# Attention scores from tile 4 on as three float32r products instead of float32 products, and the order planned anew

## Chip, core and metric

The kernel runs on one core of one Trainium2 chip. The metric is the device time of one execution, in microseconds (us); less is better. All times below are of one core.

## What is computed

Attention with rotary positions over 4 batches, 8 heads, 576 positions and a head width of 64, and behind it a two-layer feed-forward network over the 2304 tokens (512 to 2048 to 512 columns). The reference, cut to its core:

```
q_rot, k_rot = rotate(q), rotate(k)
scores = scale * (q_rot @ k_rot.T)
attn = exp(scores - max(scores))
attn = attn / (sum(attn) + 1e-9)
x = (attn @ v)                     # heads side by side: 2304 x 512
h = x @ w_in
out = (max(h, 0) + alpha * min(h, 0)) @ w_out
```

## The kernel before

**Tiles and blocks.** The 2304 tokens are cut into 18 tiles of 128; two tiles make a block, nine blocks in all. A batch has 576 tokens, that is four and a half tiles, so tiles 4 and 13 (counted from 0) lie half in one batch and half in the next. The eight heads are taken as four pairs: the two heads of a pair lie on partitions 0 to 63 and 64 to 127 of the tiles of keys (`ks`) and queries (`qn`).

**One unit of attention** is one tile and one pair of heads. `keys` (L381) and `queries` (L602) load the raw data and its rotated copy (`kraw`, `qr`), multiply both by a table (`tab`) and add them up. `pair` (L627) makes the scores on TensorE: two halves of 288 columns times two heads, each one float32 product over 64 rows of the array (L638). Tiles 4 and 13 go through `half_pair` (L650): their 64 tokens of one batch, for both heads, are laid into one 128 x 128 stationary operand with zeros in the two other quarters (L658, L660), and two float32 products of 288 columns give the scores (L666). Then, for each head (`head`): VectorE takes the maximum (L690), ScalarE the exponential (L699), the weights are split into a high and a low float16 part (L707 or L354, L716), SyncE issues a DMA that transposes them (`pt<-pp`, L720), and 14 short TensorE products with the float16 values `vv` follow (L727). The values of a batch are loaded (L412), split and copied to a second place by eight DMAs (`vv<-vv`, L455). When a tile is through, it is normalised (L771), split and transposed by a DMA (`xt<-xs`, L804).

**The network** takes a block (256 tokens) through 16 groups of 128 hidden columns: twelve float16 products into `h` (L823), the leaky rectifier (L834, L837), a split of the result in a high part `gh` and a low part `gl` (L851, L854), and six float32r products of 512 columns (L861) that add into `pair` banks: high by high, high by low, low by high. The first two blocks use float32 products there (L817, L843), while the weights are prepared; tiles 0 and 1 also do the rest of their attention in float32 (L745, L751).

**What sets the order.** Nothing runs in the order in which it is written. Each operation is recorded with a due time and the engines that may take it, with a cost for each (`op`); `Plan.run` then goes through a model of the five engines and always gives a free engine the ready operation with the earliest due time. The due times are shifted by the numbers in the table `PRM`. What comes out is a fixed list for each engine, which works it off in that order and waits where an operand isn't there. SyncE issues all DMAs, in its list's order. The lines that matter for a pair's scores on TensorE, with the cost that the plan assumes for them in ns:

```python
nc.tensor.matmul(out=ps[h]()[:, x, :HS], lhsT=qn()[r, p], rhs=kt()[r, x * HS:(x + 1) * HS], start=True, stop=True)
...
op(at, {PE: PRM["tqk"]}, scores, kind=WIDE, reads=[(qn, p // 2 * 2), kt], writes=ps)
```

Of the kernel before, what the change touches and what calls it, by code (L numbers as in the profile page):

```python
# [31 lines left out]
    [80, 75, 60, 102, 170],  # L32
    [160, 160, 160, 160, 0],
]
PRM = {"pf": 2, "pc": 3.0, "si": 3.47, "sd": 7.38, "qd": 8.0, "qd0": 3.81, "vl0": 40.33, "wl": 12.02, "wl2": 15.99, "wb": 7.7, "wb2": 0.16, "ws": -0.8, "ws2": 0.93, "kl": 23.6, "vl": 20.33, "lead": 3.61, "flow": 6, "pen": -2.44, "ph": -1.15, "xlo": 3.07, "kd": 3.61, "pl": 0.16, "wlo": 3.44, "wg": 4.0, "bk": 1500, "lead1": 1.74, "ph0": 2.99, "nb": 1, "wh": 11.0, "lw": 2.44, "pvd": 2.98, "pw": 4.01, "la": 3, "lv": 1, "nks": 5, "nvv": 5, "ka": 3.0, "va": -0.1, "vc": -2.76, "vp": 1.38, "qa": 0.46, "qr": 184.66, "tqk": 1340, "l2d": 2.62, "tl2": 1400, "nos": 2, "nr": 2, "fo": 0, "fi": 4, "gh": 9.4, "gl": 11.01, "gh0": -1.64, "gl0": 3.28, "tp": 0, "nf": 2, "sh": 2.27, "sl": 2.28, "tl": 0, "wpe": 0, "vpe": 1, "wk": 5.0}


class Buf:
# [13 lines left out]
class Tag:  # L52
    def __init__(self, pool, bufs, shape, dt, name, tag=None):
        self.pool, self.bufs, self.all, self.opened = pool, bufs, [], 0
        self.make = lambda: pool.tile(shape, dt, name=name, tag=f"{tag or name}{self.opened % bufs}")

    def new(self):
        k = len(self.all)
# [182 lines left out]
def attention_moe(ctx: ExitStack, tc: tile.TileContext, q, k, v, w_in, w_out, alpha, tab, eye, out):  # L241
# [15 lines left out]
    nc = tc.nc  # L257
# [45 lines left out]
    wus_b = single("wus", [128, 1], F32)  # L303
    wmax_b = single("wmax", [128, KC // 2, NG], F32)
    wo_pool = ctx.enter_context(tc.tile_pool(name="wo_p", bufs=1))
    ks_T = tag("ks", PRM["nks"], [128, S], F32)
    vv_T = tag("vv", PRM["nvv"], [128, 2, NSEG + NH, D], F16)
    rk_T = tag("kraw", 2, [128, 2, S], F32)
    rv_T = tag("vraw", NP, [128, 2, NH, D], F32)
    qr_T = tag("qr", 2, [128, 2, NP, 128], F32)  # L310
    qn_T = tag("qn", 2, [128, NP, 128], F32)
    st_T = tag("st", 2, [128, NP], F32)
    e_T = tag("e", 2, [128, S], F32)
    pp_T = tag("pp", 3, [128, 2, S], F16)
# [61 lines left out]
        small(at, lambda: nc.vector.reciprocal(out=dst(), in_=dst()), writes=[dst_acc])  # L376


    ks = {}

    def keys(at, b, p):  # L381
        r, t = rk_T.new(), ks_T.new()
        ks[b, p] = t
# [8 lines left out]
        op(at - PRM["ka"], {POOL: t_pool(S), DVE: (t_dve(S), slow)},  # L392
           lambda e: ENG[e].tensor_tensor(out=t(), in0=r()[:, 0], in1=r()[:, 1], op=ALU.add),
           reads=[(r, 0), (r, 1)], writes=[t])

# [204 lines left out]
    qs = {}  # L600

    def queries(at, t):  # L602
        raw, qn = qr_T.new(), qn_T.new()
        qs[t] = qn
        parts = tiles[t]
        cuts = [[0], [2]] if t == 0 else [[0, 2]]
        op(at - (PRM["qd0"] if t == 0 else PRM["qd"]), {SP: t_dma(128 * 2 * NP * 128 * 4)}, lambda e: nc.sync.dma_start(out=raw(), in_=q[t]),
           writes=[(raw, (p[2], x)) for p in parts for x in (0, 2)])
        for n, xs in enumerate(cuts):
            c, w = slice(xs[0], xs[-1] + 2), 2 * len(xs) * 128  # L610
            late = at - PRM["qa"] + 0.1 * n
# [12 lines left out]

    sums, ys, xss, vos, xt = {}, {}, {}, {}, {}

    def pair(at, step, t, b, p, a, z, banks):  # L627
        kt, vt, qn = ks[b, p], vv[b, p], qs[t]
        if z - a < 128:
            return half_pair(at, t, b, p, a, z, banks[p % 2])  # L630
        ps = [x.new() for x in banks]


        def scores(e):
# [13 lines left out]
    qds, sts = {}, {}  # L648

    def half_pair(at, t, b, p, a, z, bank):  # L650
        kt, vt, qn = ks[b, p], vv[b, p], qs[t]
        if (t, a) not in qds:
            qd, sts[t, a] = qr_T.new(), st_T.new()
            qds[t, a] = qd
            for h in range(2):
                o, c = 64 * h, 64 - 64 * h
                op(at - 2, {POOL: 420, DVE: (t_dve(256, fast=True), 1)},
                   lambda e, o=o, c=c: ENG[e].memset(qd()[o:o + 64, 0, :, c:c + 64], 0.0), writes=[(qd, h)])  # L658
                op(at - 2, {ACT: t_act(256)},
                   lambda e, o=o: nc.scalar.activation(out=qd()[o:o + 64, 0, :, o:o + 64], in_=qn()[o:o + 64, :, a:z], func=ACTF.Copy),  # L660
                   reads=[(qn, 0), (qn, 2)], writes=[(qd, 2 + h)])
# [250 lines left out]
    def attention(i):  # L912
# [116 lines left out]
```

## Time and profile before

| | us |
|---|---|
| median of 3 runs (lowest, highest) | 676.44 (675.19, 678.43) |
| profiled execution, first to last instruction | 674.6 |
| lowest run over the profiled span | 0.6 |
| TensorE (PE) busy | 643.3 |
| its weight loads (PEld), beside the products | 480.3 |
| VectorE (DVE) busy | 471.6 |
| ScalarE (ACT) busy | 338.5 |
| GpSimd (POOL) busy | 218.7 |

The profiled execution's span is the only time that is given for it; the runs' times lie up to 3.8 us above it, the median 1.8 us. Busy time of PE overlaps within itself: a product's end is modelled, and the next begins before it. So what a group of products costs is read from the starts, not from the sum of the durations. A float32 product stands in the trace as two instructions, each with a weight load of its own (512 for the 256 products of L638); a float32r product stands there as one.

### The profile page before, as it was taken

How to read it: one execution, taken by the hardware profiler on the slowest of the kernel's cores; microseconds unless marked ns; L12 is line 12 of the kernel's file. 1: busy time of each engine (PE TensorE's matmuls, PEld its weight loads, DVE VectorE, ACT ScalarE, POOL GpSimd, SP SyncE). 2: the span in 40 equal slices, each digit the busy share in tenths (PEclk: the TensorE clock that was granted, in tenths of full speed). 3: DMA queues.
4: the chain of work that ended last, by engine and by line, in shares of the span. 5: the costliest groups of instructions: out<-in, count | busy, mean ns of one | idle time of the engine just before them, and what ended most of it. 6: DMA issues, size and time to landing. Idle time of an engine off the chain costs nothing.

```text
span 674.6 us, 13695 instructions
## 1 busy us (share of the span) xinstructions
PE 643.3 (95%) x5378; PEld 480.3 (71%) x5378; DVE 471.6 (70%) x754; ACT 338.5 (50%) x752; POOL 218.7 (32%) x178
## 2 busy tenths in 40 slices
PE   1998999999999999999989999999999999999997
PEld 1577766676666667777767777788777777778775
DVE  4889799875877767587759776777766665664332
ACT  4355357653646548445634555554555544543322
POOL 3793101103476636165514221123233232211000
PEclk9999999999999999999979999999999999999999
DMA  8962885866674545658686646674865546553000
GB/s 292 329 245 97 307 249 125 195 105 149 162 201 88 121 82 120 121 137 189 148 170 116 120 87 80 114 163 93 153 129 102 88 75 102 107 100 52 32 0 32
DMA packets 185840, 90.69 MB, mean 134 GB/s; under 512 B 168624, under 2 KB 172848, under 8 KB 185776
## 3 DMA queue, kind: packets, MB, share of 16 engines
q1 hardware_dynamic: 185776, 89.82, 58.8%
q8 instruction: 42, 0.69, 0.4%
q14 instruction: 22, 0.18, 0.1%
HBM read 41.56 MB, written 4.72 MB: 69 GB/s over the span
## 4 chain that ended last, share of the span: by engine, by line
PE 85%; DMA 7%; DVE 4%; ACT 2%; issue 1%; SPq 1%; POOL 0%; ACTq 0%; DVEq 0%
PE pair L861 22%; PE h L823 21%; PE pair L638 10%; PE v L727 8%; PE h L817 8%; PE pair L843 7%; DMA pt<-pp 4%; PE pair L745 3%; PE v L751 2%; DMA kraw<-in_k_dram 2%; PE pair L666 2%; PE pair L468 1%; DVE mx L690 1%; DMA qr<-in_q_dram 1%; DMA xt<-xs 1%
## 5 line engine op out<-in xcount | busy, mean ns | idle before, releaser
L823 PE MATMUL h<-xt,wi 128*128 128x256 f16 x1344 | 175.7, 275 | 1.1 <-DMA xt<-xs 0.7
L823 PEld LDWEIGHTS <-wi 128*128 128x128 f16 x1344 | 120.1, 98 | 43.0 <-issue 28.5
L699 ACT ACTIVATE e<-pair,mx 128x576 f32<-128x576 f32 x144 | 105.8, 738 | 83.0 <-DVE mx L690 81.8
L837 DVE SCALAR_TENSOR_TENSOR r<-r,beta,h 128x256 f32<-128x256 f32 x144 | 68.8, 478 | 94.1 <-ACT r L834 93.0
L834 ACT ACTIVATE r<-h 128x256 f32<-128x256 f32 x144 | 55.2, 383 | 145.2 <-PE h L823 106.7
L690 DVE TENSOR_REDUCE mx<-pair 128x1 f32<-128x576 f32 x144 | 103.3, 751 | 25.6 <-PE pair L638 21.9
L854 POOL TENSOR_TENSOR gl<-r,gh 128x256 fp32r<-128x256 f32 x69 | 56.4, 818 | 175.6 <-ACT gh L851 152.9
L716 DVE SCALAR_TENSOR_TENSOR pp<-e,pp 128x576 f16<-128x576 f32 x128 | 102.6, 811 | 11.2 <-ACT pp L707 9.5
L861 PE MATMUL pair<-wh,gh 128*128 128x512 f32 x224 | 97.0, 433 | 0.0
L861 PE MATMUL pair<-wh,gl 128*128 128x512 f32 x224 | 88.6, 395 | 0.0
L727 PEld LDWEIGHTS <-pt 128*128 128x128 f16 (+1 forms) x2016 | 71.9, 102 | 23.0 <-issue 12.3
L861 PE MATMUL pair<-wo,gh 128*128 128x512 f32 x224 | 87.7, 391 | 0.0
L727 PE MATMUL v<-vv,pt 128*128 128x64 f16 (+1 forms) x2016 | 78.1, 195 | 4.6 <-DMA pt<-pp 4.6
L638 PE MATMUL pair<-ks,qn 64*128 64x288 f32 x512 | 82.3, 433 | 0.0
L851 ACT ACTIVATE gh<-r 128x256 fp32r<-128x256 f32 x102 | 42.5, 417 | 52.0 <-DVE r L837 26.7
L817 PE MATMUL h<-xt,wi 128*128 128x256 f32 x256 | 66.7, 392 | 1.3 <-DVE xt L788 1.2
L638 PEld LDWEIGHTS pair<-ks,qn 64*128 64x128 f32 x512 | 46.9, 189 | 23.7 <-issue 12.1
L843 PE MATMUL pair<-wo,r 128*128 128x512 f32 x128 | 60.5, 598 | 0.0
L817 PEld LDWEIGHTS h<-xt,wi 128*128 128x128 f32 x256 | 45.7, 190 | 14.9 <-issue 5.4
L707 ACT ACTIVATE pp<-e 128x576 f16<-128x576 f32 x76 | 51.4, 679 | 1.0
L861 PEld LDWEIGHTS pair<-wh,gh 128*128 128x128 f32 x224 | 42.2, 188 | 11.6 <-issue 3.1
L861 PEld LDWEIGHTS pair<-wh,gl 128*128 128x128 f32 x224 | 42.0, 187 | 10.4
(96 smaller groups left out, 715.6 us busy)
## 6 DMA issues: line engine op xcount, KB each, us to landing
kraw<-in_k_dram SPq DMA_DIRECT2D x16, 576.0 KB, 5.0
qr<-in_q_dram SPq DMA_DIRECT2D x18, 512.0 KB, 4.1
wraw<-in_moe_w_in_dram SPq DMA_DIRECT2D x16, 512.0 KB, 4.9
wraw<-in_moe_w_out_dram SPq DMA_DIRECT2D x16, 512.0 KB, 5.5
vraw<-in_v_dram SPq DMA_DIRECT2D x16, 320.0 KB, 4.1
out_dram<-os SPq DMA_DIRECT2D x18, 256.0 KB, 2.4
vv<-vv SPq DMA_DIRECT2D x32, 64.0 KB, 2.1
pt<-pp SPq DMA_TRANSPOSE x128, 3.3
```

What stands on the lines that cost most here:

```text
L638: nc.tensor.matmul(out=ps[h]()[:, x, :HS], lhsT=qn()[r, p], rhs=kt()[r, x * HS:(x + 1) * HS], start=True, stop=True)
L690: lambda e: nc.vector.tensor_reduce(out=mx()[a:z], in_=ps()[a:z, :, :HS], axis=AX.XY, op=ALU.max, negate=True),
L699: lambda e: nc.scalar.activation(out=ex()[a:z].rearrange("p (x c) -> p x c", x=2), in_=ps()[a:z, :, :HS], func=ACTF.Exp, bias=mx()[a:z], a ...
L716: lambda e: nc.vector.scalar_tensor_tensor(out=pp()[a:z, 1], in0=ex()[a:z], scalar=E_SC, in1=pp()[a:z, 0], op0=ALU.mult, op1=ALU.subtract),
L727: nc.tensor.matmul(out=v_b()[c:d, 2 * p + g], lhsT=pt()[:, s, o:o + d - c], rhs=vt()[:, g, w], start=(n == 0), stop=(n == len(order) - 1))
L817: nc.tensor.matmul(out=ps(), lhsT=w32(kk, j // FG)[:, f], rhs=x()[:, kk], start=(kk == 0), stop=(kk == KC - 1))
L823: nc.tensor.matmul(out=ps(), lhsT=wi_b()[:, kk, j // FG, w, f], rhs=x()[:, y * KC + kk], start=(kk == 0 and n == 0), stop=(kk == KC - 1 an ...
L834: lambda e: nc.scalar.activation(out=g(), in_=ps(), func=ACTF.Relu, scale=-1.0),
L837: lambda e: nc.vector.scalar_tensor_tensor(out=g(), in0=g(), scalar=beta_b()[:, j:j + 1], in1=ps(), op0=ALU.mult, op1=ALU.add),
L843: nc.tensor.matmul(out=po()[:, x], lhsT=g()[:, x * 128:(x + 1) * 128], rhs=wf[j // 2]()[:, j % 2], start=(j == 0), stop=(j == KF - 1))
L854: lambda e: ENG[e].tensor_tensor(out=gl(), in0=g(), in1=gh().bitcast(F32), op=ALU.subtract),
L861: nc.tensor.matmul(out=po()[:, x], lhsT=s()[:, ts], rhs=w, start=(j == 0 and c == 0), stop=(j == KF - 1 and c == 2))
```

## The change

From tile 4 on (`"sf": 4`) the rotated keys and queries are split after they are made: a float32r copy (the high part, on ScalarE or VectorE) and the difference to it (the low part, on GpSimd or VectorE), by the new function `in_two`. Each float32 product of the scores becomes three float32r products that add into the same bank: high by high, low queries by high keys, high queries by low keys. That holds for `pair` and for `half_pair`, whose operand `qd` now has two layers, twice the zeros and twice the copies. Tiles 0 to 3 keep the float32 products (`ks`, `qp`). Keys of batch 0 are kept in both forms; those of the later batches are added up in place in `kraw` and split into `kh`. The pool of keys has five buffers as before, each twice as large. All due times in `PRM` are new, and the plan is told 1150 ns for a pair's scores where it was told 1340, and 800 for a half pair's where it was told 980. A scratch area of the DMA descriptors is made smaller (512), which frees room in SBUF.

```diff
...
-    ks_T = tag("ks", PRM["nks"], [128, S], F32)
+    kh_T = tag("kh", PRM["nks"], [128, 2, S], F32R)
...
-    qn_T = tag("qn", 2, [128, NP, 128], F32)
+    qn_T = tag("qn", 2, [128, 2, NP, 128], F32R)
...
+    def in_two(at, acc, src, dst, n, first, second):
+
+        op(at, {ACT: t_act(n), DVE: (t_dve(n, fast=True), PRM[first])},
+           lambda e: nc.scalar.activation(out=dst()[:, 0], in_=src(), func=ACTF.Copy) if e == ACT
+           else nc.vector.tensor_copy(out=dst()[:, 0], in_=src()), reads=acc[0], writes=acc[1])
+        op(at, {POOL: t_pool(n), DVE: (t_dve(n), PRM[second])},
+           lambda e: ENG[e].tensor_tensor(out=dst()[:, 1], in0=src(), in1=dst()[:, 0].bitcast(F32), op=ALU.subtract),
+           reads=acc[0] + acc[1], writes=acc[2])
...
+    def split_keys(at, b, p):
+        t = kh[b, p] = kh_T.new()
+        src, acc = ks[b, p] if b else (ks[b, p], [ks[b, p]])
+        in_two(at - PRM["kt0" if b == 0 else "kt"], (acc, [(t, 0)], [(t, 1)]), src, t, S, "khd", "kld")
...
+        if split:
+            acc = [(raw, (p[2], x)) for p in parts for x in (0, 2)]
+            in_two(at - PRM["qt"], (acc, [(qn, 0)], [(qn, 1)]), lambda: raw()[:, 0], qn, NP * 128, "qhd", "qld")
...
+    TERMS = ((0, 0), (1, 0), (0, 1))
...
             for x in range(2):
-                for h in range(2):
-                    r = slice(64 * h, 64 * h + 64)
-                    nc.tensor.matmul(out=ps[h]()[:, x, :HS], lhsT=qn()[r, p], rhs=kt()[r, x * HS:(x + 1) * HS], start=True, stop=True)
-
-        op(at, {PE: PRM["tqk"]}, scores, kind=WIDE, reads=[(qn, p // 2 * 2), kt], writes=ps)
+                for n, (i, j) in enumerate(TERMS if split else [(0, 0)]):
+                    for h in range(2):
+                        r, c = slice(64 * h, 64 * h + 64), slice(x * HS, (x + 1) * HS)
+                        nc.tensor.matmul(
+                            out=ps[h]()[:, x, :HS], lhsT=qn()[r, i, p] if split else qn()[r, p],
+                            rhs=kt()[r, j, c] if split else kt()[r, c], start=(n == 0), stop=(n == 2 or not split))
+
+        op(at, {PE: PRM["tqs" if split else "tqk"]}, scores, kind=WIDE,
+           reads=[(qn, 0), (qn, 1), (kt, 0), (kt, 1)] if split else [(qn, p // 2 * 2), kt], writes=ps)
...
         def scores(e):
             for x in range(2):
-                nc.tensor.matmul(out=ps()[:, x, :HS], lhsT=qd()[:, 0, p], rhs=kt()[:, x * HS:(x + 1) * HS], start=True, stop=True)
-
-        op(at, {PE: 980}, scores, kind=WIDE, reads=[(qd, x) for x in range(4)] + [kt], writes=[ps])
+                for n, (i, j) in enumerate(TERMS):
+                    nc.tensor.matmul(out=ps()[:, x, :HS], lhsT=qd()[:, i, p], rhs=kt()[:, j, x * HS:(x + 1) * HS],
+                                     start=(n == 0), stop=(n == 2))
+
+        op(at, {PE: PRM["tqh"]}, scores, kind=WIDE, reads=[(qd, x) for x in range(4)] + [(kt, 0), (kt, 1)], writes=[ps])
...
+                if t >= PRM["sf"] and (b, p) not in kh:
+                    split_keys(at, b, p)
...
```

The table also changes where things stand. First place: the list of SyncE around the first heads of tile 9, where batch 2 begins. `pt<-pp` is the transpose of one head's weights, `vv<-vv` a copy of the values, `xt<-xs` the transpose of a tile for the network. Before:

```order
L720 DMA_TRANSPOSE pt<-pp 128x9x128 x3
L804 DMA_TRANSPOSE xt<-xs 128x8x128
L455 DMA vv<-vv 64x2x256 x2
L720 DMA_TRANSPOSE pt<-pp 128x9x128
L455 DMA vv<-vv 64x2x256 x6
L412 DMA vraw<-in_v_dram 128x640 x2
L720 DMA_TRANSPOSE pt<-pp 128x9x128 x2
L412 DMA vraw<-in_v_dram 128x640 x2
```

After the change, the same place:

```order
L933 DMA out_dram<-os 128x512 x2
L482 DMA vv<-vv 64x2x256 x2
L767 DMA_TRANSPOSE pt<-pp 128x9x128
L482 DMA vv<-vv 64x2x256 x3
L767 DMA_TRANSPOSE pt<-pp 128x9x128
L482 DMA vv<-vv 64x2x256 x3
L851 DMA_TRANSPOSE xt<-xs 128x8x128
L398 DMA kraw<-in_k_dram 128x1152
L767 DMA_TRANSPOSE pt<-pp 128x9x128 x2
L439 DMA vraw<-in_v_dram 128x640 x2
```

The eight copies stood as two and six, the six together with two loads between two transposes; they now stand as two, three and three, with a transpose between them, and the loads of `vraw` come later.

Second place: the list of GpSimd where the keys of batch 2 are made, among the low parts `gl` of the network (with buffer numbers). Before:

```order
L621 TENSOR_TENSOR qn_2965<-qr_2190 128x512
L854 TENSOR_TENSOR gl_2999<-r_2951,gh_2954 128x256
L854 TENSOR_TENSOR gl_3034<-r_3019,gh_3031 128x256
L393 TENSOR_TENSOR ks_3077<-kraw_1486 128x576
L854 TENSOR_TENSOR gl_3104<-r_3062,gh_3066 128x256
L854 TENSOR_TENSOR gl_3132<-r_3118,gh_3130 128x256
L390 TENSOR_TENSOR kraw_3106<-kraw_3106,tab_172 128x1152
L393 TENSOR_TENSOR ks_3185<-kraw_1579 128x576
```

After:

```order
L413 TENSOR_TENSOR kraw_3225<-kraw_3225 128x576
L901 TENSOR_TENSOR gl_3362<-r_3319,gh_3343 128x256
L393 TENSOR_TENSOR kh_3407<-kraw_3225,kh_3407 128x576
L901 TENSOR_TENSOR gl_3436<-r_3395,gh_3409 128x256
L404 TENSOR_TENSOR kraw_3398<-kraw_3398,tab_172 128x1152
L901 TENSOR_TENSOR gl_3486<-r_3438,gh_3455 128x256
L413 TENSOR_TENSOR kraw_3398<-kraw_3398 128x576
L901 TENSOR_TENSOR gl_3554<-r_3488,gh_3522 128x256
```

The sum of the two halves (now L413, into `kraw` itself) is followed by a further operation for the low part (`kh<-kraw,kh`, L393 of the new file). In the whole list GpSimd gets 13 such operations on keys and 12 on queries (`qn<-qr,qn`, 128x512); VectorE gets 3 and 2, ScalarE 16 copies of keys and 14 of queries.

## Rows read from the trace of the kernel before

**Rows 1.** Page, parts 1 and 2: engines' busy time; PE's busy tenths in 40 slices.
```profile
PE 643.3 (95%) x5378; PEld 480.3 (71%) x5378; DVE 471.6 (70%) x754; ACT 338.5 (50%) x752; POOL 218.7 (32%) x178
PE   1998999999999999999989999999999999999997
```
**Rows 2.** Page, part 4: the chain that ended last, by engine.
```profile
PE 85%; DMA 7%; DVE 4%; ACT 2%; issue 1%; SPq 1%; POOL 0%; ACTq 0%; DVEq 0%
```
**Rows 3.** PE's waits: total us, times, longest.
```profile
PE pair L368 <- DVE cr L367: 10.8, 1, 10.8
PE v L727 <- DMA pt<-pp: 4.6, 5, 2.9
PE pair L468 <- DVE dg L354: 3.5, 1, 3.5
```
**Rows 4.** Timeline at 299.8 us, a pair's scores: start, length, engine and instructions.
```profile
299.58 0.38 PE L823 MATMUL h<-xt,wi 128*128 128x256 f16 x2
299.89 0.79 PEld L638 LDWEIGHTS pair<-ks,qn 64*128 64x128 f32 x8 [0.21 <-issue]
299.89 1.24 PE L638 MATMUL pair<-ks,qn 64*128 64x288 f32 x8
301.06 0.50 PE L861 MATMUL pair<-wh,gh 128*128 128x512 f32 x1
301.40 0.39 PE L861 MATMUL pair<-wo,gh 128*128 128x512 f32 x1
301.40 0.19 PEld L861 LDWEIGHTS pair<-wh,gl 128*128 128x128 f32 x1
...
302.33 0.40 PE L861 MATMUL pair<-wh,gl 128*128 128x512 f32 x1
```
**Rows 5.** Scores by form: busy us, mean ns of one instruction.
```profile
L638 PE MATMUL pair<-ks,qn 64*128 64x288 f32 x512 | 82.3, 433 | 0.0
...
L666 PE MATMUL pair<-ks,qr 128*128 128x288 f32 x64 | 18.1, 407 | 0.0
```
**Rows 6.** Timeline at 178 us, two half pairs' scores, back to back.
```profile
178.25 2.10 PE L666 MATMUL pair<-ks,qr 128*128 128x288 f32 x8
```
**Rows 7.** Helpers by form: busy us, mean ns of one.
```profile
L621 POOL TENSOR_TENSOR qn<-qr 128x512 f32<-128x512 f32 x16 | 21.0, 1315 | 86.4 <-PE pair L638 82.7 <-PE pair L666 3.6
...
L393 POOL TENSOR_TENSOR ks<-kraw 128x576 f32<-128x576 f32 x11 | 17.9, 1623 | 21.6 <-PE pair L666 19.2 <-PE pair L638 2.4
...
L393 DVE TENSOR_TENSOR ks<-kraw 128x576 f32<-128x576 f32 x5 | 6.5, 1311 | 0.0
...
L707 ACT ACTIVATE pp<-e 128x576 f16<-128x576 f32 x76 | 51.4, 679 | 1.0
```
**Rows 8.** Timeline at 333 us, SyncE's queue at the start of batch 2.
```profile
332.88 1.34 SPq L804 DMA_TRANSPOSE xt<-xs  x1
334.31 1.28 SPq L455 DMA_DIRECT2D vv<-vv  x2
335.75 1.29 SPq L720 DMA_TRANSPOSE pt<-pp  x1
337.14 4.70 SPq L455 DMA_DIRECT2D vv<-vv  x6
341.89 1.08 SPq L412 DMA_DIRECT2D vraw<-in_v_dram  x2
343.08 3.64 SPq L720 DMA_TRANSPOSE pt<-pp  x2
```
**Rows 9.** Timeline of PE, 344 to 355 us and at 88 us.
```profile
347.62 0.93 PE L727 MATMUL v<-vv,pt 128*128 128x64 f16 x14 [2.87 <-DMA pt<-pp]
348.36 2.75 PE L823 MATMUL h<-xt,wi 128*128 128x256 f16 x12
...
353.84 1.48 PE L823 MATMUL h<-xt,wi 128*128 128x256 f16 x12
...
88.40 0.92 PE L817 MATMUL h<-xt,wi 128*128 128x256 f32 x3 [1.20 <-DVE xt L788]
```
**Rows 10.** Busy us by stretch; after POOL's: granted clock, DMA share, GB/s.
```profile
347.00:354.00 7.00, 6.38 (x50) 4.67 (x51) 2.61 (x6) 0.80 (x2) 1.25 (x2) 0.53 0.73 175
...
88.40:95.00 6.60, 6.60 (x28) 4.42 (x29) 6.57 (x9) 4.33 (x11) 0.00 (x0) 1.00 0.87 194
```
**Rows 11.** Timeline at 11 us: GpSimd and VectorE at the same time.
```profile
10.92 3.85 POOL L390 TENSOR_TENSOR kraw<-kraw,tab 128x576 f32<-128x576 f32 x2
...
13.43 1.42 DVE L354 TENSOR_SCALAR dg<-eye,vs 128x128 f32<-128x128 f32 x1
```

More of the change, by code (lines that the diff above doesn't have):

```diff
@@ L54, in __init__ @@
         self.pool, self.bufs, self.all, self.opened = pool, bufs, [], 0
-        self.make = lambda: pool.tile(shape, dt, name=name, tag=f"{tag or name}{self.opened % bufs}")
+        self.name = tag or name
+        self.make = lambda: pool.tile(shape, dt, name=name, tag=f"{self.name}{self.opened % bufs}")
     def new(self):
@@ L376, in scale_of, with plain @@
         small(at, lambda: nc.vector.reciprocal(out=dst(), in_=dst()), writes=[dst_acc])
-    ks = {}
+    ks, kh = {}, {}
+    def plain(pool_tag, buf, shape, name):
+        buf.make = lambda: pool_tag.pool.tile(shape, F32, name=name, tag=f"{pool_tag.name}{pool_tag.opened % pool_tag.bufs}")
+        return buf
+    def in_two(at, acc, src, dst, n, first, second):
[5 more added lines that the diff above has]
+           reads=acc[0] + acc[1], writes=acc[2])
     def keys(at, b, p):
-        r, t = rk_T.new(), ks_T.new()
-        ks[b, p] = t
+        r = rk_T.new()
         op(at - PRM["kl"], {SP: t_dma(128 * 2 * S * 4)}, lambda e: nc.sync.dma_start(out=r(), in_=k[b, p]),
@@ L391, in keys @@
                reads=[tab_b], writes=[(r, y) for y in x])
-        op(at - PRM["ka"], {POOL: t_pool(S), DVE: (t_dve(S), slow)},
-           lambda e: ENG[e].tensor_tensor(out=t(), in0=r()[:, 0], in1=r()[:, 1], op=ALU.add),
-           reads=[(r, 0), (r, 1)], writes=[t])
+        if b == 0:
+            t = ks[b, p] = plain(kh_T, kh_T.new(), [128, S], "ks")
+            out, acc = t, [t]
+        else:
+            out, acc = lambda: r()[:, 0], [(r, 0)]
+            ks[b, p] = (out, acc)
+        op(at - PRM["ka"], {POOL: t_pool(S), DVE: (t_dve(S), slow)},
+           lambda e: ENG[e].tensor_tensor(out=out(), in0=r()[:, 0], in1=r()[:, 1], op=ALU.add),
+           reads=[(r, 1)] if b else [(r, 0), (r, 1)], writes=acc)
+        if b == 0:
+            ks[b, p] = t
+    def split_keys(at, b, p):
+        t = kh[b, p] = kh_T.new()
+        src, acc = ks[b, p] if b else (ks[b, p], [ks[b, p]])
+        in_two(at - PRM["kt0" if b == 0 else "kt"], (acc, [(t, 0)], [(t, 1)]), src, t, S, "khd", "kld")
     vv, vraw, vs, xu = {}, {}, {}, {}
@@ L602, in queries @@
     def queries(at, t):
+        split = t >= PRM["sf"]
         raw, qn = qr_T.new(), qn_T.new()
+        if not split:
+            plain(qn_T, qn, [128, NP, 128], "qp")
         qs[t] = qn
@@ L619, in queries @@
                    reads=[tab_b], writes=[(raw, (a, x)) for x in xs])
+            to = (lambda c=c: raw()[:, 0, c]) if split else (lambda c=c: qn()[:, c])
+            acc = [(raw, (p[2], x)) for p in parts for x in xs]
             op(late, {POOL: t_pool(w), DVE: (t_dve(w), PRM["qr"])},
-               lambda e, c=c: ENG[e].tensor_tensor(out=qn()[:, c], in0=raw()[:, 0, c], in1=raw()[:, 1, c], op=ALU.add),
-               reads=[(raw, (p[2], x)) for p in parts for x in xs], writes=[(qn, x) for x in xs])
+               lambda e, c=c, to=to: ENG[e].tensor_tensor(out=to(), in0=raw()[:, 0, c], in1=raw()[:, 1, c], op=ALU.add),
+               reads=[] if split else acc, writes=acc if split else [(qn, x) for x in xs])
+        if split:
+            acc = [(raw, (p[2], x)) for p in parts for x in (0, 2)]
+            in_two(at - PRM["qt"], (acc, [(qn, 0)], [(qn, 1)]), lambda: raw()[:, 0], qn, NP * 128, "qhd", "qld")
     sums, ys, xss, vos, xt = {}, {}, {}, {}, {}
+    TERMS = ((0, 0), (1, 0), (0, 1))
     def pair(at, step, t, b, p, a, z, banks):
-        kt, vt, qn = ks[b, p], vv[b, p], qs[t]
+        vt, qn = vv[b, p], qs[t]
         if z - a < 128:
@@ L656, in half_pair @@
                 o, c = 64 * h, 64 - 64 * h
[L657 to L661, printed above, removed]
+                op(at - 2, {POOL: 840, DVE: (t_dve(512, fast=True), 1)},
+                   lambda e, o=o, c=c: ENG[e].memset(qd()[o:o + 64, :, :, c:c + 64].bitcast(F32), 0.0), writes=[(qd, h)])
+                op(at - 2, {ACT: t_act(512)},
+                   lambda e, o=o: nc.scalar.activation(
+                       out=qd()[o:o + 64, :, :, o:o + 64], in_=qn()[o:o + 64, :, :, a:z].bitcast(F32), func=ACTF.Copy),
+                   reads=[(qn, 0), (qn, 1)], writes=[(qd, 2 + h)])
         qd, ps = qds[t, a], bank.new()
@@ L1014 @@
     laid = _lay_out(inputs)
[L1015 removed]
+    nc = _bacc.Bacc("TRN2", target_bir_lowering=False, num_devices=1, dynamic_dma_scratch_size=512)
     arrays, args = {}, []
```

8 lines of the change are left out of this document (5 added, 3 removed).

## The prediction, as it was put on record

> **What bounds the kernel now.** The page first: PE is busy 643.3 of 674.6 us, and in 40 slices only the first is nearly empty [rows 1]. That alone could be a bad sign, since busy time of PE is modelled, so the chain that ended last comes next: 85% of it is PE, the rest small pieces [rows 2]. PE's own waits, third, are few: 10.8 and 3.5 us at the start, then mainly 4.6 us in five waits for the transposes of the weights, one of them 2.9 us [rows 3]. So from the first products on, time taken off PE's work comes off the total, unless something else gets late.
>
> **What the scores cost on PE.** I read starts, not durations. A pair's scores begin at 299.89 and the next product at 301.06: 1.17 us for eight float32 instructions [rows 4]. The half pair gives the price of one: eight in a row last 2.10 us, the last one 0.407 (mean, [rows 5]), so (2.10 - 0.407) / 7 = 0.242 us from start to start [rows 6]. Eight of them one after another would be 1.94 us; since a pair takes 1.17, its two heads run side by side, as four steps of 0.242 and 0.20 us for getting in and out. That the eight weight loads fit in 0.79 us says the same [rows 4]. A half pair is four instructions, 0.97 us, all in a row.
>
> One float32 product of 288 columns is thus two steps, 0.484 us, in both forms. In its place come three float32r products. No row shows one of 288 columns, nor one on half the array. The nearest is L861, float32r with 512 columns on the whole array: four starts from 301.40 to 302.33, 0.2325 us each [rows 4]. Scaled by columns that is 0.131 us. From below: half of a float32 step, 0.121 (at the full 2.4 GHz, 288 columns are 0.120). From above: at the float32 step's rate 512 columns would be 0.215, so L861 carries 0.0175 more; if that is fixed and doesn't shrink with the columns, 0.121 + 0.0175 = 0.139. I take 0.131, the middle of both.
>
> A score product then saves 0.484 - 3 x 0.131 = 0.091 us, between 0.067 and 0.121. Either unit has two such products in sequence (two halves of 288 columns; the heads are side by side or in one operand), so it saves 0.182 us, between 0.134 and 0.242. Getting in and out stays. Counted: tiles 4 to 17 are 14, of which two are split, so 12 x 4 = 48 pairs and 2 x 2 x 4 = 16 half pairs, 64 units. **64 x 0.182 = 11.6 us less PE work, between 8.6 and 15.5.**
>
> **Weight loads.** Each float32r product loads its own weights: twelve loads a pair, against eight now. A load lasts 0.19 us, longer than a step of 0.131. I cost it at nothing: at 301.40 a load begins together with a product, and products follow at 0.2325 [rows 4], so loads run under the product before them; that they also do so at 0.131 is covered only by the pair's own loads, which begin two at a time and fit eight in 0.79 us, 0.10 per load of one row half even if they came in no more than two rows [rows 4].
> By the Trainium skill, "TensorE: Matmul & The Clock Gate", part 3, a weight load overlaps with a running product only if it goes to other rows of the array; this speaks against a change that adds loads, and it is a rival below. By it L861 would need 0.19 + 0.215 = 0.40 us a product, and the row has 0.2325.
>
> **The splits.** Added are 16 splits of keys and 14 of queries: 30 copies and 30 differences. By the lists GpSimd gets 13 + 12 of the differences: 13 x 1.62 + 12 x 1.32 = 37 us; VectorE 5, at most 1.31 each, 7 us; ScalarE 30 copies at up to 0.68, 20 us (the first two prices are of the additions of the same shapes, the last of a copy of 576) [rows 7]. That brings GpSimd from 218.7 to 256 us, VectorE from 471.6 to 478, ScalarE from 338.5 to 359, against some 658: 39, 73 and 55% [rows 1]. The zeros and copies for the half pairs double, eight of each, a microsecond or two in all. I cost all of it at nothing, since PE's work lies over it and the lists place splits between older work. If that cover is gone, a late split is a copy and a difference, 0.68 + 1.62 = 2.3 us of waiting; behind it in GpSimd's list stands a `gl`, for which the next L861 waits.
> GpSimd's operations also hold up VectorE: at 13.43 a tiny scaling of 128 columns took 1.42 us and ended at 14.85, just after two GpSimd operations ended at 14.77 [rows 11]. So the 37 us may cost VectorE up to 37 us more, at worst 515 us, 78% of 658.
> The Trainium skill, "SBUF — State Buffer", "Who interferes with whom", calls this an exclusive lock on a shared pair of ports for a whole instruction. The row agrees. By that rule alone all 37 us would be VectorE's loss; by PE's chain the sum stays as it is.
>
> **The new order.** The largest wait inside the kernel is 2.87 us at 344.75, for a transpose [rows 9]. What is late there is SyncE's queue: the transpose is issued at 343.08, behind six copies of the values (4.70 us) and two loads (1.08), 5.78 us without one transpose [rows 8]. The wait costs more than itself: in the 7 us from 347 on the granted clock is 0.53, so PE is mostly at 1.2 GHz (twelve products take 2.75 us, elsewhere 1.48), and loses 7 x 0.47 = 3.3 us [rows 9, 10]. After the change three copies (3 x 0.78), one `xt` transpose (1.34) and one load (some 0.54) stand in that gap: 4.2 us, 1.6 less. The wait then shrinks to 1.3. A wait of 1.20 us at 87 us left the clock at 1.00 [rows 9, 10], so I count the clock's loss as gone too. **1.6 + 3.3 = 4.9 us**, between 0 (the same wait in another place) and 6.2 (both gone wholly). At the start of batch 1 and in tile 13 long runs of copies remain in the new list; before, such runs stood there too, and the other four waits for transposes are 1.7 us together [rows 3], so I leave them at nothing. The start of the program, up to the first float32 scores, has the same order on PE.
>
> **The sum.** Profiled span 674.6 - 11.6 - 4.9 = 658.1 us. The runs' median of 676.4 lies 1.8 over that span, so the runs should give **660 us**. By the bounds: 674.6 + 1.8 - 15.5 - 6.2 = 654.7 and 676.4 - 8.6 - 0 = 667.8.
>
> **Rivals.**
> - *The helpers get late* (the other sign). PE waits for `kh` or `qn`, or for weights or `gl` that VectorE and GpSimd deliver later. For it: VectorE already waits behind GpSimd [rows 11], and is the second engine by load [rows 1]. Against: over the whole kernel it has a quarter of its time free, and PE's list has waits of under 5 us on data now [rows 3]. Price: 2.3 us for each of 30 splits; the gain of 16.5 is used up at seven full waits, and beyond that the kernel is slower. Ten give 676.4 - 16.5 + 23 = 683; two or three, which I think more likely within this case, about 666.
> - *The heads don't run side by side in float32r.* Twelve steps of 0.131 and 0.20 are 1.77 us, 0.60 more than now: 48 x 0.60 - 16 x 0.182 - 4.9 = 21, so 697. Against it is only that the float32 instructions do run side by side on the same rows [rows 4].
> - *The loads don't hide.* Six steps of 0.19 + 0.121 = 0.311 are 1.87 us where four of 0.242 were 0.97: 64 x 0.90 = 57.6, less 4.9: 729. Against it stand L861's starts [rows 4].
> - *The order gains nothing*, and only PE's work shrinks: 676.4 - 11.6 = 665.
>
> **Chances.** Forecast with its bounds, 654.7 to 667.8, the order's case in it: 0.79 (order without gain 0.25 of that). Helpers late 0.14, half of it below 673. Heads in sequence 0.05. Loads 0.02. The range for 8 in 10: from 654 to 669. What a measurement can tell from no change is about 0.5%, 3.4 us: faster is below 673.0, slower above 679.8. Faster 0.79 + 0.07 = 0.86; the same 0.05; slower 0.02 + 0.05 + 0.02 = 0.09.
>
> **What would show it.** Right: the scores' starts in the new trace 0.12 to 0.14 us apart, in twos, a pair's scores some 0.99 us up to the next product (0.93 to 1.04), a half pair's 0.79; the wait at the start of tile 9 under 1.5 us and the clock at 1.00 there; GpSimd near 256 us. Wrong: starts of 0.26 or more for twos (heads in sequence) or 0.31 (loads); waits of PE for `kh`, `qn` or `gl` that add up to over 5 us; a new stretch with a clock near 0.5, which would cost half its length.

## The result and the profile after

The changed kernel takes **668.52 us** (median of four runs, 666.49 to 669.46) against 677.39 us for the kernel before, run beside it: a ratio of 0.987, with a 95% interval of 0.984 to 0.990. Measured again beside the kernel before, it gave 0.982 (0.979 to 0.985). So it is faster by 9 to 12 us, where 16.5 were forecast; 668.5 lies at the upper edge of the range (654 to 669) and 0.7 above the forecast's own upper bound of 667.8. The profiled execution spans 664.7 us, 9.9 less than the one before.

Part 1 of the page after, busy time by engine:

```profile
PE 630.3 (95%) x5602; PEld 487.4 (73%) x5602; DVE 496.2 (75%) x752; ACT 359.4 (54%) x784; POOL 271.2 (41%) x208
```

PE is busy for 13.0 us less than in [rows 1]. PE's waits after (total us, times, longest), those that the text needs:

```profile
PE v L774 <- DMA pt<-pp: 3.6, 3, 2.4
...
PE v L831 <- DVE y L818: 2.3, 1, 2.3
PE h L864 <- DVE r L884: 1.7, 2, 1.0
...
PE h L870 <- DVE r L884: 0.8, 1, 0.8
```

The same view of the kernel before has for `y` and for the rectified part `r`:

```profile
PE v L784 <- DVE y L771: 0.8, 1, 0.8
...
PE h L823 <- DVE r L837: 0.4, 1, 0.4
```

Two things are to be seen. The wait for the transposes, on which the new order's gain rested, is still there: 2.4 us in one piece where [rows 3] has 2.9, 3.6 in all where they have 4.6. And VectorE is waited for longer: `y` 2.3 instead of 0.8 us, `r` 2.5 instead of 0.4. In all PE stands idle for 34.4 us of its span where it was 31.3, 3.1 us more; with 13.0 less of busy time that is the 9.9 us of span.

**The scores** came out as forecast. PE's timeline after, a pair and the product behind it, and then the products of the network ahead of a half pair and those behind the group that follows it:

```profile
305.54 1.05 PE L678 MATMUL pair<-kh,qn 64*128 64x288 f32 x12
306.53 1.48 PE L870 MATMUL h<-xt,wi 128*128 128x256 f16 x12
```
```profile
431.22 0.82 PE L870 MATMUL h<-xt,wi 128*128 128x256 f16 x6
...
434.06 0.83 PE L870 MATMUL h<-xt,wi 128*128 128x256 f16 x6
```

From the pair's start to the next product are 0.99 us, where [rows 4] have 1.17. Inside a pair the products start in twos, and from the second two on they follow at 0.13 us (median of the 48 pairs). How the half pair does is seen below, beside the same place with float32 products.

**The start of batch 2.** SyncE's list after, then PE at the same time, then the windows there (the columns of [rows 10]):

```profile
324.83 1.95 SPq L482 DMA_DIRECT2D vv<-vv  x3
326.88 1.30 SPq L767 DMA_TRANSPOSE pt<-pp  x1
328.23 1.94 SPq L482 DMA_DIRECT2D vv<-vv  x3
330.26 1.28 SPq L851 DMA_TRANSPOSE xt<-xs  x1
331.59 0.57 SPq L398 DMA_DIRECT2D kraw<-in_k_dram  x1
332.27 4.05 SPq L767 DMA_TRANSPOSE pt<-pp  x2
```
```profile
337.25 0.58 PE L774 MATMUL v<-vv,pt 128*128 128x64 f16 x14 [2.38 <-DMA pt<-pp]
338.27 0.58 PE L774 MATMUL v<-vv,pt 128*128 128x64 f16 x14 [0.44 <-DMA pt<-pp]
```
```profile
334.00:341.00 7.00, 4.18 (x42) 3.17 (x40) 3.70 (x4) 1.70 (x5) 4.75 (x3) 0.84 0.93 232
341.00:348.00 7.00, 7.00 (x60) 5.29 (x58) 5.25 (x8) 3.79 (x9) 2.89 (x3) 0.92 0.70 160
```

From the end of the issue of one transpose of weights (328.18) to the start of the next (332.27) are 4.1 us, as the prediction had worked out (4.2, before 5.78). Yet PE waits 2.38 + 0.44 = 2.82 us, as long as before (2.87). SyncE is busy without a break from 322.46 on, where one more transpose of weights stands ahead of the lines shown. So what should count is when that whole run begins and how much stands in it: six of the eight copies stand in it, the other two just ahead. That the copies are what makes it too long is tested below. The clock loses 7 x 0.16 + 7 x 0.08 = 1.7 us, half of the 3.3 of [rows 10]. That half is all that the new order brought here.

**The helpers.** GpSimd and VectorE by form, after (busy us, mean ns of one):

```profile
L393 POOL TENSOR_TENSOR qn<-qr,qn 128x512 fp32r<-128x512 f32 x12 | 16.3, 1355 | 51.2 <-ACT qn L390 51.2
L393 POOL TENSOR_TENSOR kh<-kraw,kh 128x576 fp32r<-128x576 f32 x9 | 15.5, 1726 | 13.2 <-ACT kh L390 13.2
...
L393 POOL TENSOR_TENSOR kh<-ks,kh 128x576 fp32r<-128x576 f32 x4 | 6.6, 1652 | 14.2 <-ACT kh L390 14.2
```
```profile
L763 DVE SCALAR_TENSOR_TENSOR pp<-e,pp 128x576 f16<-128x576 f32 x128 | 119.2, 945 | 6.4 <-ACT pp L754 5.2
...
L393 DVE TENSOR_TENSOR kh<-kraw,kh 128x576 fp32r<-128x576 f32 x3 | 4.0, 1331 | 0.0
...
L393 DVE TENSOR_TENSOR qn<-qr,qn 128x512 fp32r<-128x512 f32 x2 | 2.0, 1010 | 0.0
```

The differences cost GpSimd 16.3 + 15.5 + 6.6 = 38.4 us (37 forecast); the rest of its 52.5 us more is work that the new lists gave it. VectorE's five differences cost 6.0 us (7 forecast), and its other instructions became longer: the 128 of L763 took 811 ns each before, 102.6 us in all.

### The profile page after: what moved, and what is told of

It reads as the page before. It is cut to its first block, busy times and chain, and to the rows that moved or that the text cites. A ratio compares the mean times of both kernels' runs of the same rounds, so it can differ in the third digit from the quotient of the medians.

```text
span 664.7 us, 14239 instructions
## 1 busy us (share of the span) xinstructions
PE 630.3 (95%) x5602; PEld 487.4 (73%) x5602; DVE 496.2 (75%) x752; ACT 359.4 (54%) x784; POOL 271.2 (41%) x208
## 4 chain that ended last, share of the span: by engine, by line
PE 83%; DVE 7%; DMA 5%; ACT 2%; issue 1%; SPq 1%; POOL 0%; ACTq 0%; DVEq 0%
PE pair L908 24%; PE h L870 22%; PE pair L678 9%; PE v L774 9%; PE pair L890 7%; PE h L864 6%; PE pair L792 3%; DMA kraw<-in_k_dram 2%; DMA pt<-pp 1%; PE v L798 1%; PE pair L712 1%; DVE mx L737 1%; DMA qr<-in_q_dram 1%; DVE pp L763 1%; ACT e L746 1%
## 5 line engine op out<-in xcount | busy, mean ns | idle before, releaser
L870 PE MATMUL h<-xt,wi 128*128 128x256 f16 x1344 | 171.7, 273 | 0.9 <-DVE r L884 0.8
L763 DVE SCALAR_TENSOR_TENSOR pp<-e,pp 128x576 f16<-128x576 f32 x128 | 119.2, 945 | 6.4 <-ACT pp L754 5.2
L737 DVE TENSOR_REDUCE mx<-pair 128x1 f32<-128x576 f32 x144 | 103.3, 751 | 21.6 <-PE pair L678 20.0
L881 ACT ACTIVATE r<-h 128x256 f32<-128x256 f32 x144 | 54.9, 381 | 102.6 <-PE h L870 83.0
L901 POOL TENSOR_TENSOR gl<-r,gh 128x256 fp32r<-128x256 f32 x63 | 54.2, 860 | 133.1 <-ACT gh L898 86.6
L774 PE MATMUL v<-vv,pt 128*128 128x64 f16 (+1 forms) x2016 | 80.5, 194 | 3.9 <-DMA pt<-pp 3.6
L898 ACT ACTIVATE gh<-r 128x256 fp32r<-128x256 f32 x93 | 38.7, 416 | 49.2 <-PE pair L908 29.9
L864 PE MATMUL h<-xt,wi 128*128 128x256 f32 x256 | 62.9, 386 | 2.4 <-DVE r L884 1.7
L890 PE MATMUL pair<-wo,r 128*128 128x512 f32 x128 | 62.0, 606 | 0.0
L754 ACT ACTIVATE pp<-e 128x576 f16<-128x576 f32 x81 | 54.7, 679 | 2.5 <-ACT e L746 0.9
L678 PE MATMUL pair<-kh,qn 64*128 64x288 f32 x576 | 51.0, 309 | 0.0
L678 PEld LDWEIGHTS pair<-kh,qn 64*128 64x128 f32 x576 | 39.9, 186 | 11.0 <-issue 4.0
```

The lines of the kernel that those rows point to most:

```text
L678: nc.tensor.matmul(out=ps[h]()[:, x, :HS], lhsT=qn()[r, i, p] if split else qn()[r, p], rhs=kt()[r, j, c] if split else kt()[r, c], start= ...
L737: lambda e: nc.vector.tensor_reduce(out=mx()[a:z], in_=ps()[a:z, :, :HS], axis=AX.XY, op=ALU.max, negate=True),
L754: lambda e: nc.scalar.activation(out=pp()[a:z, 0], in_=ex()[a:z], func=ACTF.Copy, scale=1.0 if early else E_SC) if e == ACT
L763: lambda e: nc.vector.scalar_tensor_tensor(out=pp()[a:z, 1], in0=ex()[a:z], scalar=E_SC, in1=pp()[a:z, 0], op0=ALU.mult, op1=ALU.subtract),
L774: nc.tensor.matmul(out=v_b()[c:d, 2 * p + g], lhsT=pt()[:, s, o:o + d - c], rhs=vt()[:, g, w], start=(n == 0), stop=(n == len(order) - 1))
L864: nc.tensor.matmul(out=ps(), lhsT=w32(kk, j // FG)[:, f], rhs=x()[:, kk], start=(kk == 0), stop=(kk == KC - 1))
```

## The experiments

All times are medians beside runs of the kernel before on the same chip, which gave 680 to 682 us in these three sets; the ratios are what can be compared. "After" without a further word is the changed kernel.

**The new table alone.** The kernel before, with float32 products and no splits, planned with the new table.

```diff
-PRM = {"pf": 2, "pc": 3.0, "si": 3.47, "sd": 7.38,
...
+PRM = {"pf": 2, "pc": 3.12, "si": 3.2, "sd": -0.06,
...
```

> The kernel before with its float32 score products, planned by the new table of due times. Theory (the gain is the cheaper products, the new order by itself is worth little): 675 to 678 us, as the kernel before. Rival (the order carries most of the 8.9 us): 668 to 671. If the order costs something by itself (longer waits at the start, a late VectorE), it comes out over 678.

Measured: 696.47 us, ratio 1.024 (1.018 to 1.029). The theory and the rival are both missed by some 20 us; only the third case, an order that costs something by itself, has the sign right. PE's waits, and windows at the start:

```profile
PE v L727 <- DMA pt<-pp: 9.0, 3, 4.4
PE pair L745 <- ACT e L699: 9.0, 6, 3.3
```
```profile
49.00:56.00 7.00, 7.00 (x32) 6.01 (x32) 5.61 (x6) 1.82 (x3) 0.00 (x0) 0.50 0.31 96
56.00:63.00 7.00, 5.16 (x21) 3.69 (x18) 4.23 (x8) 2.78 (x6) 1.74 (x2) 0.50 0.74 278
```

VectorE's list there:

```profile
34.63 3.13 DVE L516 SCALAR_TENSOR_TENSOR wi<-wraw,wi 128x1024 int32<-128x1024 int32 x1
37.69 1.89 DVE L511 TENSOR_SCALAR wi<-wraw 128x1024 int32<-128x1024 int32 x1
39.50 3.63 DVE L520 SCALAR_TENSOR_TENSOR wi<-wraw,wi 128x1024 int32<-128x1024 int32 x1
43.06 1.41 DVE L690 TENSOR_REDUCE mx<-pair 128x1 f32<-128x576 f32 x2
```

The maxima (L690) of the next two heads stand behind three steps of unpacking weights, 8.4 us; `e` comes late, PE waits 3.3 us, and the clock is at half for most of the 20 us that follow: the two windows cost at most 7 us, and those on either side of them (0.66 and 0.87) at most another 3.3, less where PE stands idle in them. So this table, given the old list of operations, is a loss; whether another table would gain with them is not shown.

**The new products in the old table.** After, with the old value for every entry that both tables have; the entries for the splits stay.

```diff
-PRM = {"pf": 2, "pc": 3.12, "si": 3.2, "sd": -0.06,
...
+PRM = {"pf": 2, "pc": 3.0, "si": 3.47, "sd": 7.38,
...
```

> The changed kernel with its float32r products and splits, but every due time that both tables have from the table of before. Theory (the products save 64 x 0.18 = 11.4 us wherever PE is the bound): 664 to 668 us, at least as good as the changed kernel. Rival (the splits need the new order, else the helpers get late): 672 or more, with waits of PE on keys, queries or the rectifier of over 5 us.

Measured: 697.47 us, ratio 1.026 (1.020 to 1.031). The rival came true.

```profile
PE v L774 <- DMA pt<-pp: 13.0, 11, 2.8
...
PE h L870 <- DVE r L884: 6.8, 7, 2.5
PE h L864 <- DVE r L884: 3.9, 4, 1.4
```

PE's busy time, 640.1, is 3.2 us under [rows 1], with the scores' saving of 11.6 in it; part of that goes to the clock (0.51 from 189 to 196 us). And PE stands idle for 23 us more than before the change, most of it for the transposes (13.0 against 4.6) and for `r` (10.7 against 0.4). Either table costs 2.4 to 2.6% with the other kernel's operations, and the change as a whole gains 1.3 to 1.8%: table and operations have to fit each other. What the order of the changed kernel is worth by itself, the next run tells.

**float32 products in the new order.** After, instruction for instruction in the same order, splits made; the scores are one float32 product of the high parts. It leaves out what the low parts add.

```diff
-    TERMS = ((0, 0), (1, 0), (0, 1))
+    TERMS = ((0, 0),)
...
-                            out=ps[h]()[:, x, :HS], lhsT=qn()[r, i, p] if split else qn()[r, p],
+                            out=ps[h]()[:, x, :HS], lhsT=qn()[r, i, p].bitcast(F32) if split else qn()[r, p],
...
```

> The changed kernel in its own order with all its splits, but the scores from tile 4 on are again one float32 product each, of the high parts alone (the low parts are made and left out of the scores). Theory (in one and the same order the products alone are worth 64 x 0.184 = 11.8 us): 679 to 682 us, a pair's scores 1.17 us again. Rival (with so many splits and waits the saved PE time is partly idle anyway): 670 to 676.

Measured: 679.18 us, ratio 0.997 (0.995 to 1.000), span 676.3. The same half pair as above:

```profile
438.71 0.82 PE L870 MATMUL h<-xt,wi 128*128 128x256 f16 x6
...
441.74 0.83 PE L870 MATMUL h<-xt,wi 128*128 128x256 f16 x6
```

From the products ahead of the half pair to those behind the group that follows it are 3.03 us here and 2.84 after: 0.19 saved, where 0.182 was forecast (over all 16 the median is 0.18). A pair takes 1.17 again up to the next product, 0.18 more than after. The spans differ by 676.3 - 664.7 = 11.6 us, which is the forecast of 64 x 0.182. These are single executions; by the ratios (0.997 against 0.982 to 0.987) the two kernels are 7 to 10 us apart. And this kernel is about as fast as the one before, so its order is no loss: new order and splits with the old products are worth 0 to 0.5%. The theory held.

**Only the product of the high parts.** After, with one float32r product instead of three, the low parts left out; it asks how much more a faster PE would bring.

```diff
-    TERMS = ((0, 0), (1, 0), (0, 1))
+    TERMS = ((0, 0),)
...
```

> The changed kernel in its own order, but only the first of the three products (high by high); the two with low parts are left out. Theory (PE is the bound everywhere behind the start): 64 units x 4 steps x 0.131 = 33.5 us less, 634 to 637 us. Rival (VectorE and the transposes are close behind PE): only a part of it comes, 645 to 657, and PE's waits for transposes and the rectifier grow by the rest.

Measured: 654.22 us, ratio 0.960 (0.957 to 0.963), span 652.9.

```profile
PE v L774 <- DMA pt<-pp: 8.7, 11, 3.4
PE h L870 <- DVE r L884: 6.9, 8, 2.4
PE h L864 <- DVE r L884: 3.6, 3, 2.0
```

A pair takes 0.46 us up to the next product (295.87 to 296.33), 0.53 less; over 64 units some 33 us of work, of which 12 (by spans) to 16 us arrive (by medians, against the 669.71 of the version with the heads apart in the same set, below). The theory fell, and the rival's range holds the time. The rest turned into waits for the same two things, the transposes and `r` (19.2 us, after 6.1), and half-clock stretches behind them. Behind PE the helpers stand close.

**No low parts made.** After, in the same order, but the 30 differences are not computed, and all three products read the high parts.

```diff
-           lambda e: ENG[e].tensor_tensor(out=dst()[:, 1], in0=src(), in1=dst()[:, 0].bitcast(F32), op=ALU.subtract),
+           lambda e: None,
...
-    TERMS = ((0, 0), (1, 0), (0, 1))
+    TERMS = ((0, 0), (0, 0), (0, 0))
...
```

> The changed kernel in its own order, but the 30 differences (low parts) are not computed on GpSimd and VectorE, and the three products all take the high parts; PE, the copies and the order stay. Theory (the differences on GpSimd hold up VectorE, and that is part of what was missing): 664 to 667 us, with VectorE's L763 back from 945 to near 811 ns and PE's waits for the rectifier (2.5 us) mostly gone. Rival (they are hidden): 668 to 669, within 0.2% of the changed kernel.

Measured: 669.22 us, ratio 0.981 (0.976 to 0.986): no gain over the changed kernel, as the rival had it. VectorE:

```profile
L763 DVE SCALAR_TENSOR_TENSOR pp<-e,pp 128x576 f16<-128x576 f32 x128 | 112.4, 890 | 9.2 <-ACT pp L754 7.9
```

GpSimd loses 39 us (271.2 to 232.1), and VectorE's busy time falls by 17.1 (496.2 to 479.1). Of these, 6.0 are its own five differences, which are gone too; the other 11 are instructions that became shorter, 6.8 of them in this line, which came down to 890 ns and not near 811. (Against another execution of the changed kernel, below, in which VectorE was busy for 501.9 us, it is 16.) The splits do hold VectorE up, but PE's time hides that: the prediction's price of nothing holds, within the 3 us or so by which executions differ.

**No copies of the values in batch 2.** After, in the same order; the eight copies of batch 2 are left out, and the products read other blocks of the values.

```diff
+                    (lambda e: None) if b == 2 else
                    lambda e, t=t, i=i: nc.sync.dma_start(
...
-                    out=v_b()[c:d, 2 * p + g], lhsT=pt()[:, s, o:o + d - c], rhs=vt()[:, g, w],
+                    out=v_b()[c:d, 2 * p + g], lhsT=pt()[:, s, o:o + d - c], rhs=vt()[:, g, w - NH if b == 2 and NH <= w < NSEG else w],
```

> The changed kernel in its own order, but the eight copies of the values of batch 2 are left out (the products of that batch read other value blocks in their place). Theory (transposes at the start of tile 9 are late because of the copies in SyncE's queue and on the DMA engines): the wait of 2.4 us there is under 0.5, the clock stays at 1.00, 664 to 666 us. Rival (the load of keys and the xt transpose ahead of it are enough to make it late): the wait stays over 1.5 us, 667 to 669.

Measured: 664.54 us, ratio 0.976 (0.972 to 0.980), span 660.9. SyncE and the windows:

```profile
328.56 0.58 SPq L398 DMA_DIRECT2D kraw<-in_k_dram  x1
330.20 3.30 SPq L768 DMA_TRANSPOSE pt<-pp  x2
```
```profile
334.00:341.00 7.00, 7.00 (x76) 5.64 (x75) 6.33 (x7) 3.73 (x10) 4.70 (x4) 1.00 0.66 154
```

SyncE now has free time ahead of the transposes (329.14 to 330.20), PE waits for none at this place, and the clock stays at 1.00, as the theory had it. The copies are the cause of this wait.

**The copies issued by ScalarE.** All work of after, in its order; only the engine that issues the eight copies is another.

```diff
-                   lambda e, t=t, i=i: nc.sync.dma_start(
+                   lambda e, t=t, i=i: (nc.scalar if b == 2 else nc.sync).dma_start(
```

> The changed kernel in its own order, but the eight copies of the values of batch 2 are issued by ScalarE, at the same place in the plan, instead of SyncE; nothing is left out. Theory (the transposes at the start of tile 9 are late because SyncE's list makes them wait behind the copies): as without the copies, a wait under 0.7 us there and 4 to 6 us less than the changed kernel, 662 to 665. Rival (the DMA engines are what is full, whoever issues): the wait stays near 2.4 us, 667 to 670; if ScalarE itself is held up by the copies, over 670.

Measured: 667.81 us, ratio 0.980 (0.977 to 0.983). By its time that is the rival's range, 667 to 670, and no clear gain; yet in its trace PE waits for no transpose at this place. So it was run once more, beside the changed kernel:

> The version in which ScalarE issues the eight copies of values of batch 2, once more beside the changed kernel. Theory (SyncE's list in its order makes the transposes late; the wait of 2.8 us and 1.7 us of lost clock go): 4 to 5 us under the changed kernel of the same job. Rival (what is won there is given back at the next waits, for the rectifier or for later transposes): within 2 us of it.

> The changed kernel once more, so that the version with copies issued by ScalarE can be compared with it on one chip. It stood at 0.987 of the kernel before. Expected 0.982 to 0.990, the wait for the transposes at tile 9 (2.4 us and 0.4 us) again at the same place, since the order is fixed. If the half-clock stretches move from execution to execution, the profile's span may be up to 3.4 us away from 664.7 with the same waits.

Measured: changed kernel 668.69 us (666.10 to 669.53), ratio 0.982 (0.979 to 0.985); with copies by ScalarE **663.27 us** (660.92 to 667.93), ratio 0.975 (0.972 to 0.979). SyncE and PE of the second run:

```profile
331.80 2.97 SPq L767 DMA_TRANSPOSE pt<-pp  x2
```
```profile
331.12 1.47 PE L870 MATMUL h<-xt,wi 128*128 128x256 f16 x12 [1.40 <-DVE r L884]
```

The copies move the same bytes, and the wait for the transposes at this place is gone (the next products of weights and values start at 336.75 without one): it is the place in SyncE's list that made them late. That the transfers add nothing to it is not fully separated: ScalarE issues the last copy 1 to 3 us earlier by PE's progress. In the changed kernel's own trace of this set the wait is 2.3 us at this place.

The gain is 5.4 us between these medians, though the runs' spreads overlap. What belongs to this place is read more safely from the traces, since PE works through the same list in all these versions. The same two groups of products, after and with the copies by ScalarE (second run):

```profile
330.89 1.06 PE L678 MATMUL pair<-kh,qn 64*128 64x288 f32 x12
...
342.78 1.49 PE L870 MATMUL h<-xt,wi 128*128 128x256 f16 x12
```
```profile
332.93 1.07 PE L678 MATMUL pair<-kh,qn 64*128 64x288 f32 x12
...
340.13 1.49 PE L870 MATMUL h<-xt,wi 128*128 128x256 f16 x12
```

From the one to the other are 11.9 us after, and 11.3 to 12.9 in the three other executions with these products and the copies in SyncE's list (the changed kernel again, no low parts, heads apart). They are 7.2 us without the copies and in all three executions with copies by ScalarE (both runs here and the next version). The difference of 4.7 is the wait of 2.8 and 1.9 of clock. Just ahead of this stretch, the three executions with copies by ScalarE have a wait for `r` of 1.1 to 1.4 us that the others don't have, so a little over 3 us are left as gain at this place. What else lies between the times, as between 667.81 and 663.27 for one and the same kernel, arises at other places and differs from execution to execution.

**All copies by ScalarE.**

```diff
-                   lambda e, t=t, i=i: nc.sync.dma_start(
+                   lambda e, t=t, i=i: (nc.scalar if b > 0 else nc.sync).dma_start(
```

> As the version before, but the copies of values of batches 1 to 3 are all issued by ScalarE. Theory (SyncE's list is what makes transposes late, elsewhere too): the rest of the waits for transposes goes, under 1 us beyond copies_act2, since in the changed kernel's trace such waits outside tile 9 are under 1 us together. Rival (ScalarE, which delivers e and the transposed input, is held up by issuing and its copies wait for data of the values): PE waits for e or for the rectified weights more, and the time is 1 to 4 us above copies_act2.

Measured: 670.51 us, ratio 0.983 (0.979 to 0.987). The theory fell, the rival had the sign right but 1 to 4 us as the size: it is 7 us above the version with batch 2 alone.

```profile
PE v L774 <- DMA vv<-vv: 1.6, 1, 1.6
```

The 1.6 us is a new wait, for a copy of the values itself, at the start of batch 1 (182 us), and behind it the clock is at 0.76 for 7 us. From the lists, what ScalarE has ahead of it there issues the copy too late; that was not tried. Together this is 2.6 of the 7 us, by the same products around it in both traces; the rest arises elsewhere.

**The heads apart.** After, with the three products of head 0 written ahead of those of head 1.

```diff
-                for n, (i, j) in enumerate(TERMS if split else [(0, 0)]):
-                    for h in range(2):
+                for h in range(2):
+                    for n, (i, j) in enumerate(TERMS if split else [(0, 0)]):
```

> The changed kernel in its own order, but within a pair the three products of one head stand ahead of the three of the other, instead of taking turns. Theory (products start in the order in which they stand, and two run side by side only if they stand next to each other and take other rows): nine steps instead of six in a pair, 48 x 3 x 0.131 = 19 us more, 685 to 690, a pair's scores some 1.38 us. Rivals: no overlap at all, twelve steps, 704 to 708; or PE takes them side by side in any order, 667 to 670.

Measured: 669.71 us, ratio 0.983 (0.979 to 0.986). A pair:

```profile
309.24 1.06 PE L678 MATMUL pair<-kh,qn 64*128 64x288 f32 x12
310.24 1.49 PE L870 MATMUL h<-xt,wi 128*128 128x256 f16 x12
```

1.00 us for twelve products: in sequence they would need 12 x 0.131 + 0.20 = 1.77. The theory that only products written next to each other run side by side fell.

## Why the prediction came out 8.5 us too low

- **The scores on PE: right, in place and size.** The step of 0.131 us, the two heads side by side and 0.20 for getting in and out gave 0.99 a pair and 0.182 saved a unit; measured are 0.99 and 0.18 to 0.19, and 11.6 us between single executions of the two kernels in one order. The loads did hide: products follow at 0.13 us, and a load lasts 0.19 [rows 4]. Only the 0.79 us named for a half pair was low, 0.88 up to the next product (median of the 16).
- **The new order: the step that failed.** "The wait then shrinks to 1.3 ... I count the clock's loss as gone too. 1.6 + 3.3 = 4.9 us." The wait measured 2.38 + 0.44 = 2.82, the clock's loss 1.7: of 4.9 us 1.7 came. The gap between two transposes did shrink as worked out. But, as the lists read, the wait is the time from the first copy to the last transpose needed, less the time that PE takes to get there; the count left out the copies that stood on the other side of a transpose. That the copies in SyncE's list make the wait and the clock loss is shown: without them there, or with them in ScalarE's list, the same products take 7.2 us where they took 11.9. The prediction's lower bound, "the same wait in another place", had the wait right.
- **Waits that the prediction left at nothing.** New waits, 1.5 us more for `y` at 54.8 us and 2.1 more for `r`, took back twice what the clock gave; some other waits became shorter, and 3.1 us more of idle time are left. The prediction said that the program's start "has the same order on PE"; it has, but VectorE's list is another. After, it holds at that place:

```profile
52.92 0.68 DVE L538 TENSOR_SCALAR wi<-wraw 128x1024 int32<-128x1024 int32 x1
53.52 2.29 DVE L543 SCALAR_TENSOR_TENSOR wo<-wraw,wo 128x1024 int32<-128x1024 int32 x1
...
56.40 0.68 DVE L818 TENSOR_TENSOR y<-v,rs 128x512 f32<-128x512 f32 x1
```

  Two steps of unpacking weights stand ahead of `y`, one of them 2.29 us long. That they are the cause is read from the list, and was not tried; the list alone doesn't set the size, since in the other executions with this order the wait is 0.8 to 2.2 us. The waits for `r` remain with fewer low parts (2.6 us in the kernel without differences), so the splits' load is not what makes them.
- **The splits at nothing: right for the total, wrong for VectorE.** It was busy for 496 us, not 478: 24.6 us more, within the worst case of 515. Its own differences are 6.0 of that, and some 11 to 16 is what the 38.4 us of differences on GpSimd cost it; that all of GpSimd's time would be VectorE's loss, as the prediction put it at worst, was too much. The rest comes with the new lists: with the new table and no splits at all VectorE was busy for 496.7 us.
- **The rivals.** "The order gains nothing" had 665, and two or three late helpers 666; both came true in part. Heads in sequence (697) and loads that don't hide (729) didn't. That the table has to fit the operations was in none of them: with the old table the helpers are late, and the kernel takes 697 us.
- **The remaining 2 us** are the base: 1.8 us lay between run and span for before and after alike, but the profiled execution was the fastest of the four runs (666.49 against the median of 668.52).
- **The signs, and luck.** Of the signs named as right, the scores' came; the wait under 1.5 us and the clock at 1.00 at the start of tile 9 did not (2.82; 0.84 and 0.92), and GpSimd had 271 us, not 256. That the time is lower follows from the scores, as forecast. That 668.5 still lies within the range, by half a microsecond, is luck: two thirds of the order's term are missing, and waits that no term held are in it.

By spans: 674.6 - 13.0 (some 11.3 of work and 1.7 of clock) + 3.1 (idle time) = 664.7.

## What to carry to other kernels

When a wait sits behind an engine's list that is kept in order, count everything from the first item of the busy run to the one needed, against the time the waiting engine needs to get there; here a shorter gap inside the run changed nothing. Time taken off the bounding engine arrives only as far as its inputs come earlier too: of the 33 us that one product in place of three saved, 12 to 16 arrived. A table of due times belongs to its list of operations: each table was a loss with the other's, so the price of the products shows only when they are exchanged in one fixed order. And a transfer that delays others only by its place in a list can be issued by another engine, but only where that engine is early enough.

## What the runs showed of the hardware

- TensorE ran products on the upper and the lower half of its rows side by side though all of one half were written ahead of the other's: 1.00 us a pair, against 0.99 when written in turns. Whether the engine itself pairs them is not shown.
- A wait does not always cost clock. Behind the wait of 2.3 us for `y` (after) the granted clock stayed at 1.00; in the version with copies by ScalarE (second run) 1.3 us at the same place were followed by a window at 0.79:

```profile
56.00:63.00 7.00, 7.00 (x45) 6.30 (x45) 4.77 (x5) 3.93 (x7) 0.81 (x1) 0.79 0.23 76
```

  That is 7 x 0.21 = 1.5 us. It differs between executions of one order: the changed kernel, run again, had two stretches at half clock between 49 and 63 us (0.76 over the 14 us), one behind a wait of 1.2 us for `e` and one behind 1.5 us for `y`, and lost 3.4 us. What decides it stays open.
- GpSimd's work stretches some of VectorE's: 38.4 us of differences less on GpSimd gave VectorE 11 to 16 us back beside its own differences, 0.3 to 0.4 us for each. L763, which reads two tiles, took 945 and 977 ns in two executions of the changed kernel and 890 without the differences; the maximum (L737) took 751 and 750. The Trainium skill, "SBUF — State Buffer", "Who interferes with whom", has an exclusive lock on a pair of ports that the two engines share, held for a whole instruction, and only those of VectorE's instructions that use the pair, such as those with two inputs in SBUF, contend for it. The direction agrees, and so does a share well under one.
